# Reordering the start and the pair scalings of a fused retention + Mish MLP kernel on one core

## The chip, the cores and the metric

One NeuronCore of a Trainium2 chip. The metric is the time of one execution on the device in microseconds (us), the median of the fast runs. The mean granted clock of TensorE (1.0 is full speed) is given where it matters. TensorE is called PE, VectorE DVE, ScalarE ACT, GpSimd POOL.

## The reference

```python
# q, k, v: (8, 8, 576, 64) fp32;  moe_w_in (512, 2048), moe_w_out (2048, 512)
scores = (1 / sqrt(64)) * q @ k.transpose(0, 1, 3, 2)
gamma  = 1 - 2.0 ** (-5 - arange(8))                      # one decay per head
rel    = pos[:, None] - pos[None, :]                      # pos = arange(576)
ret    = scores * where(rel >= 0, gamma[:, None, None] ** rel, 0)
x      = (ret @ v) -> (4608, 512)                         # 8 heads x 64 side by side
h      = x @ w_in                                         # "G1"
g      = h * tanh(softplus(h))                            # Mish
out    = g @ w_out                                        # "G2"
```

## The kernel before

The 4608 rows of x are made in 36 chunks of 128, two chunks a pair. For a chunk the kernel scales q and k by powers of the decay (step P, DVE, two TENSOR_TENSORs), transposes them on PE and copies them out of PSUM, the memory that PE writes its results to (T), multiplies q by k and masks (S), multiplies by v and casts into `xT` (O). For the first two pairs k is also turned back on PE into `ks` (`step_n`), and products of k and v are summed up from chunk to chunk (`step_k`) for later O steps. In calls of `first`, q and k stand for scaling, Q and K for the transposes with their copy, V for a cast of v. Four chunks are a tile t: `g1(t, f)` makes one of 16 groups of h and ACT takes Mish of it into `gT`; `g2(t, i)` is a quarter of one chunk's product with w_out. The first four chunks take another way (`first`), with the rows of four tokens on one partition, because it lets the loads start earlier. Chunks 0 to 15 are transposed on PE; the later ones by DMA, and nothing of that part changes. The attention steps stand between the G1 and G2 groups by hand: the program order on each engine is the order of the calls. PSUM has two `sc` buffers of 4 KB, one `st`, two `hp` of 2 KB (all of G1, some of G2) and one `ops` of 2 KB.

```python
def turn_first(n, i):                       # transposes of q (i=0) or k (i=1) of chunk n
    ...
    if n < NCH - 1:
        tp = ps_h.tile([P, 4, P], BF16, name="hp")
    else:                                   # chunk 3: q and k are two parts of one sc tile
        if "tp" not in r:
            r["tp"] = ps_sc.tile([P, 4, NP, P], BF16, name="sc")
        tp = r["tp"][:, 2 * i]
    ... 4 transposes ...
    nc.scalar.copy(r["qk"][:, i, u]..., tp...)

def step_t(n):                              # transposes of chunk n: 4 of q, 4 of k, one tile
    ...
    tp = ps_sc.tile([P, 4, NP, P], BF16, name="sc")[:, 0:2]
    for i in range(2):
        ... nc.tensor.transpose(tp[:, i, p, :], flat[:, ts(p, P)], ident)
    nc.scalar.copy(r["qk"][:, :, u], tp)

def g2(t, i):                               # hp or ops takes the result; DVE copies it to res
    s, part = divmod(i, 4)
    ...
        if t == nT - 1 and s % 2 == 0 or (t, s) in ((0, 1), (0, 3), (1, 1)):
            outs[t] = ps_h.tile([P, d_model], F32, name="hp")
        else:
            outs[t] = ps_o.tile([P, d_model], F32, name="ops")
    ...
    if part == 3:
        store(t, s, ops, nc.vector.tensor_copy)

def visit(m, w):                            # pair m (4 to 7) spread over 8 groups, w = 0 to 7
    n = 2 * m
    if w == 0:
        step_p(m)
        if 2 * m + 2 < NPE: load(m + 4)
    elif w == 2: ...; one(n, "T")
    elif w == 3: one(n + 1, "T")
    elif w == 5: one(n, "S"); one(n + 1, "S")
    elif w == 7: step_k(m); one(n, "O"); one(n + 1, "O")

for i in range(nF):                         # visits 4, 5, 6, 7 and what they stand between
    if i >= 8: visit(4, i % 8)
    g2(0, i)
for i in range(8):
    visit(5, i); g2(1, i)
for i in range(nF):
    visit(6 + i // 8, i % 8)
    ...
    g1(2, i)
    if i % 2: g2(1, 8 + i // 2)
```

## Time and profile before

| | before |
|---|---|
| time, median of 3 runs | 320.43 us (319.65 to 320.83) |
| span of the profiled execution | 318.9 us |
| mean granted clock of PE | 1.0 |
| PE busy | 303.3 us |
| PE not busy | 15.6 us, some 6.5 of it before 10 us and after the last matmul |

PE is the engine to watch. A line of a timeline gives start, duration, engine, line of the program, operation, output and inputs, shapes, the number of instructions drawn together, and in brackets how long the engine stood idle before it and what released it. Because the ends of matmuls are modelled, a loss is counted here as in the prediction: the step from one start to the next, less the same step where nothing waits (0.86 us for four 128x512 matmuls, 0.89 for sixteen 128x128, 0.44 for a chunk's eight transposes). The chain that ended last reads in before:

```profile
PE 78%; DMA 9%; DVE 4%; issue 3%; SPq 2%; POOL 2%; ACT 1%; POOLq 0%; DVEq 0%
```

(SPq is SyncE's queue, POOLq and DVEq those of POOL and DVE; "issue" is time in which nothing was waited for that the profile shows.) These shares count the whole length of each step of the chain, and not the time that PE waited: PE itself waited 0.77 us for w_in, at 22.93. The waits of PE for loads, copies and scalings are what the change goes after.

### The profile page before, as it was taken

How to read it: one execution, taken by the hardware profiler on the slowest of the kernel's cores; microseconds unless marked ns; L12 is line 12 of the kernel's file. 1: busy time of each engine (PE TensorE's matmuls, PEld its weight loads, DVE VectorE, ACT ScalarE, POOL GpSimd, SP SyncE). 2: the span in 40 equal slices, each digit the busy share in tenths (PEclk: the TensorE clock that was granted, in tenths of full speed). 3: DMA queues.
4: the chain of work that ended last, by engine and by line, in shares of the span. 5: the costliest groups of instructions: out<-in, count | busy, mean ns of one | idle time of the engine just before them, and what ended most of it. 6: DMA issues, size and time to landing. Idle time of an engine off the chain costs nothing.

```text
span 318.9 us, 6061 instructions
## 1 busy us (share of the span) xinstructions
PE 303.3 (95%) x2607; PEld 159.1 (50%) x2644; DVE 132.9 (42%) x177; ACT 129.3 (41%) x214; POOL 78.5 (25%) x101
## 2 busy tenths in 40 slices
PE   6779899989999999999999999999999999999995
PEld 2346488745555555444545454445454544444444
DVE  6641554047558475444454535353626232001111
ACT  5656666412464542343434343424242432333200
POOL 6676762532440311313121222240000000000000
PEclk9999999999999999999999999999999999999999
DMA  6999999999998594959594959495040400000032
GB/s 169 261 186 219 198 209 221 202 230 194 247 178 104 110 188 101 168 130 177 121 184 114 182 116 194 106 172 127 33 101 33 101 33 35 33 33 35 33 81 84
DMA packets 71946, 43.38 MB, mean 136 GB/s; under 512 B 55664, under 2 KB 63088, under 8 KB 71920
## 3 DMA queue, kind: packets, MB, share of 16 engines
q0 software_dynamic: 43424, 26.22, 55.7%
q1 hardware_dynamic: 28352, 16.65, 20.3%
q8 instruction: 20, 0.33, 0.4%
q10 hardware_dynamic: 144, 0.13, 0.1%
q14 instruction: 6, 0.05, 0.0%
HBM read 36.70 MB, written 9.44 MB: 145 GB/s over the span
## 4 chain that ended last, share of the span: by engine, by line
PE 78%; DMA 9%; DVE 4%; issue 3%; SPq 2%; POOL 2%; ACT 1%; POOLq 0%; DVEq 0%
PE hp L381 31%; PE ops L419 30%; DMA v<-in_v_dram 5%; PE hp L419 3%; PE sc L317 3%; DVE qks L280 3%; DMA w_in_t<-in_moe_w_in_dram 3%; PE hp L404 2%; SPq L137 2%; PE sc L366 2%; PE sc L359 2%; DMA kraw<-in_k_dram 2%; PE st L338 2%; PE sc L296 1%; PE hp L431 1%
## 5 line engine op out<-in xcount | busy, mean ns | idle before, releaser
L383 ACT ACTIVATE gT<-hp 128x512 bf16<-128x512 f32 x122 | 72.9, 598 | 126.1 <-PE hp L381 105.9
L381 PE MATMUL hp<-xT,w_in_t 128*128 128x512 bf16 x460 | 121.2, 380 | 1.1 <-ACT gT L406 0.2
L419 PE MATMUL ops<-w_out_t,gT 128*128 128x512 bf16 x475 | 121.3, 379 | 0.7
L419 PEld LDWEIGHTS <-gT 128*128 128x128 bf16 x560 | 54.2, 98 | 64.7 <-issue 0.8
L439 DVE COPY res<-ops 128x512 f32<-128x512 f32 x30 | 20.8, 692 | 129.7 <-PE ops L419 129.7
L381 PEld LDWEIGHTS <-w_in_t 128*128 128x128 bf16 x488 | 45.2, 98 | 52.3 <-issue 0.6
L320 DVE TENSOR_TENSOR sm<-sc,mask 128x1024 bf16<-128x1024 f32 x36 | 42.6, 1217 | 23.7 <-PE sc L317 23.7
L564 POOL COPY seen<-qkT 1x1 bf16<-1x1 bf16 x10 | 1.8, 177 | 127.0 <-DMA qkT<-qks 127.0
L342 ACT ACTIVATE ssb<-st,diag 128x512 bf16<-128x512 f32 x32 | 20.2, 684 | 15.5 <-PE st L338 15.5
L107 POOL DMA_DIRECT2D qraw<-in_q_dram x16 | 17.2, 1076 | 24.3 <-DVE qks L280 20.3
L370 DVE CAST xT<-sc 128x512 bf16<-128x512 f32 x32 | 20.8, 685 | 5.4 <-PE sc L366 4.5
L280 DVE TENSOR_TENSOR qks<-kraw,gk 128x1024 bf16<-128x1024 f32 (+1 forms) x18 | 19.8, 1098 | 0.0
L280 DVE TENSOR_TENSOR qks<-qraw,gq 128x1024 bf16<-128x1024 f32 (+1 forms) x18 | 19.7, 1096 | 0.0
L107 POOL DMA_DIRECT2D kraw<-in_k_dram x16 | 17.2, 1076 | 6.1 <-DVE sm L320 3.7
L419 PE MATMUL hp<-w_out_t,gT 128*128 128x512 bf16 x77 | 18.3, 379 | 0.4 <-issue 0.3
L107 POOL DMA_DIRECT2D v<-in_v_dram x16 | 17.3, 1086 | 4.2 <-DMA kraw<-in_k_dram 2.5
L297 ACT COPY qkT<-sc 128x1024 bf16<-128x1024 bf16 x12 | 12.2, 1013 | 14.1 <-PE sc L296 13.9
L404 PE MATMUL hp<-xT,w_in_t 128*128 128x128 bf16 x280 | 17.2, 219 | 0.0
L404 PEld LDWEIGHTS <-w_in_t 128*128 128x128 bf16 x280 | 15.8, 98 | 0.7 <-issue 0.2
L366 PE MATMUL sc<-sm,v 128*64 128x128 bf16 x288 | 13.8, 220 | 0.4 <-DVE sm L320 0.4
L406 ACT ACTIVATE gT<-hp 128x512 bf16<-128x512 f32 (+1 forms) x18 | 10.4, 586 | 6.5 <-PE hp L404 6.2
L317 PEld LDWEIGHTS <-qkT 64*128 64x128 bf16 x288 | 8.1, 94 | 9.8 <-issue 5.9
(72 smaller groups left out, 157.1 us busy)
## 6 DMA issues: line engine op xcount, KB each, us to landing
out_dram<-res SPq DMA_DIRECT2D x31, 256.0 KB, 3.4
qraw<-in_q_dram POOLq DMA_DIRECT2D x12, 512.0 KB, 6.2
kraw<-in_k_dram POOLq DMA_DIRECT2D x12, 512.0 KB, 7.5
v<-in_v_dram POOLq DMA_DIRECT2D x12, 256.0 KB, 8.0
qraw<-in_q_dram POOLq DMA_DIRECT2D x8, 256.0 KB, 9.7
kraw<-in_k_dram POOLq DMA_DIRECT2D x8, 256.0 KB, 9.5
w_out_t<-in_moe_w_out_dram POOLq DMA_DIRECT2D x4, 512.0 KB, 11.6
qraw<-in_q_dram SPq DMA_DIRECT2D x8, 128.0 KB, 4.1
```

Of the source, the lines that this page charges most:

```text
L107: nc.gpsimd.dma_start(out=r[x][ds(off, ni)].rearrange("p u h d -> p (u h) d"), in_=src[ds(b, 2), :, ds(i0, ni), :].rearrange("b h p d -> p ...
L280: nc.vector.tensor_tensor(r["qks"][:, i, u], r["qk"[i]][:, u], g, op=OP.mult)
L317: nc.tensor.matmul(sc[:, e, p, :], lhsT=qk[r, 1, u, p, :], rhs=qk[r, 0, u, p, :], start=True, stop=True)
L320: nc.vector.tensor_tensor(sm.rearrange("p e n i -> p (e n) i"), sc.rearrange("p e n i -> p (e n) i"), (mask if len(chunks[n]) == 1 else ma ...
L342: nc.scalar.activation(ssb[:, :, :, e, :], st, AX.Copy, scale=diag[:, e:e + 1])
L366: nc.tensor.matmul(ot[ds(64 * e, 64), p, :], lhsT=vs[:, u, 2 * p + e, :], rhs=sm[:, e, p, :], start=(start and p == 0), stop=True, skip_gr ...
L370: (nc.scalar.copy if t == 0 else nc.vector.tensor_copy)(xts[t][:, :, ts(s, P)], ot)
L381: nc.tensor.matmul(hp, lhsT=w_in_t[:, c, ts(f, P)], rhs=xts[t][:, c, :], start=(c == 0), stop=(c == KC - 1))
L383: nc.scalar.activation(gts[t][:, f, :], hp, AX.Mish)
L404: nc.tensor.matmul(hp[:, j, :], lhsT=w_in_t[:, c, ts(f + j, P)], rhs=xts[t][:, c, ts(s, P)], start=(c == 0), stop=(c == KC - 1))
L419: nc.tensor.matmul(ops, lhsT=gts[t][:, f, ts(s, P)], rhs=w_out_t[:, f, :], start=(f == 0), stop=(f == nF - 1))
L439: copy(ot, ops)
```

## The change

Its intent: PE should find its operands ready. Chunk 3's transposes go ahead of the first G1 groups, with Q copied by ACT and K by DVE; chunks 4 to 7 have their copies split over the two engines; a pair's scaling is issued one visit (eight groups) ahead of its transposes; the second quarter of w_in comes in two loads. The diff, cut to its core:

```diff
+        copy = nc.vector.tensor_copy if n == NCH - 1 and i else nc.scalar.copy     # turn_first
-        nc.scalar.copy(r["qk"][:, :, u], tp)                                       # step_t
+        if n < 2 * NCH:
+            nc.scalar.copy(r["qk"][:, 0, u], tp[:, 0])
+            nc.vector.tensor_copy(r["qk"][:, 1, u], tp[:, 1])
+        else:
+            nc.scalar.copy(r["qk"][:, :, u], tp)
...
-    load_w_in(4, 4)
+    load_w_in(4, 2)
+    load_w_in(6, 2)
...
+    first(3, "q")
     first(2, "S")
     first(1, "O")
-    first(3, "q")
-    keep_warm(4)
+    first(3, "V")
+    keep_warm(3)
     first(2, "O")
-    first(3, "k")
-    steps = {0: "Q", 1: "KV", 2: "S", 4: "O"}
-    for f in range(6):
+    first(3, "kQK")
+    for f in range(4):
         g1_some(0, f, NCH - 1)
-        first(3, steps.get(f, ""))
+        first(3, {0: "S", 2: "O"}.get(f, ""))
     g1_chunk(3, 0)
-    g1_chunk(3, 4, 2)
...                                     # steps of pair 2 one or two groups earlier or later
     def visit(m, w):
         if w == 0:
-            step_p(m)
             if 2 * m + 2 < NPE: load(m + 4)
...
             one(n, "O")
             one(n + 1, "O")
+            if 2 * m + 2 < NPE:
+                step_p(m + 1)
...
-        if i >= 8:
+        if i == 6:
+            step_p(4)
+        elif i >= 8:
             visit(4, i % 8)
         g2(0, i)
...
-        if i == 6:
+        if i == 9:
             step_p(8)
-        elif i == 8:
+        elif i == 11:
             cross(8)
```

More of the change, by code (lines that the diff above doesn't have):

```diff
@@ L262, in turn_first @@
             nc.tensor.transpose(tp[:, t, :], lines[:, ts(t, P)], ident)
-        nc.scalar.copy(r["qk"][:, i, u].rearrange("p n (g t) -> p n g t", t=4),
-                       tp.rearrange("p t (g n) -> p n g t", n=NP))
+        copy = nc.vector.tensor_copy if n == NCH - 1 and i else nc.scalar.copy
+        copy(r["qk"][:, i, u].rearrange("p n (g t) -> p n g t", t=4), tp.rearrange("p t (g n) -> p n g t", n=NP))
     def cast_first(n):
@@ L492 @@
     load(5)
+    first(3, "q")
     first(2, "S")
     first(1, "O")
-    first(3, "q")
-    keep_warm(4)
+    first(3, "V")
+    keep_warm(3)
     first(2, "O")
-    first(3, "k")
-    steps = {0: "Q", 1: "KV", 2: "S", 4: "O"}
-    for f in range(6):
+    first(3, "kQK")
+    for f in range(4):
         g1_some(0, f, NCH - 1)
-        first(3, steps.get(f, ""))
+        first(3, {0: "S", 2: "O"}.get(f, ""))
     g1_chunk(3, 0)
-    g1_chunk(3, 4, 2)
-    for i in range(6, nF):
-        if i == 7:
+    for i in range(4, nF):
+        if i == 5:
             step_n(0)
+        elif i == 7:
+            step_k(0)
         elif i == 9:
-            step_k(0)
-        elif i == 10:
             step_n(1)
@@ L519 @@
             one(4, "O")
-            one(5, "T")
         g1(0, i)
@@ L527 @@
                 if fb == 0:
+                    one(n + 1, "T")
+                elif fb == 1:
                     one(n + 1, "S")
@@ L530 @@
                         step_k(n // 2)
-                elif fb == 1 and n < 6:
+                elif fb == 2 and n < 6:
                     one(n + 2, "P")
-                elif fb == 2:
+                elif fb == 3:
                     one(n + 1, "O")
-                elif fb == 3 and n < 6:
-                    one(n + 2, "T")
             g1_chunk(n, 4 * fb)
```

## The prediction

> **What bounds the kernel now.** I first read the page's busy shares, to see which engine fills the span:
>
> ```profile
> PE 303.3 (95%) x2607; PEld 159.1 (50%) x2644; DVE 132.9 (42%) x177; ACT 129.3 (41%) x214; POOL 78.5 (25%) x101
> ```
>
> TensorE is busy 303.3 of 318.9 us and the change takes no real matmul away, so all it can win is PE idle time: at most 15.6 us, of which some 2.9 lie in the first 10 us and 3.6 after the last matmul, both untouched. The ends of matmuls are modelled (a 128x512 one shows 380 ns, yet four take 0.86 us start to start), which hides up to 0.2 us of each gap; so I count losses as the step from one start to the next, less the step of the same group where nothing waits. The waits of the whole run say that PE never waits long in one place, so I read the timeline of PE, then of the engines it waits for, stage by stage.
>
> The start (timeline, all engines):
>
> ```profile
> 16.99 0.41 PE L366 MATMUL sc<-sm,v 128*64 128x128 bf16 x8
> 18.08 0.81 PE L392 MATMUL hp<-xT,w_in_t 128*128 128x384 bf16 x4 [0.67 <-ACT xT L370]
> ...
> 19.31 0.58 ACT L264 COPY qkT<-sc 128x512 bf16<-128x512 bf16 x1
> ...
> 19.94 0.38 PE L262 MATMUL sc<-ident,qks 128*128 128x128 bf16 x4 [0.18 <-ACT qkT L264]
> ...
> 22.93 0.82 PE L392 MATMUL hp<-xT,w_in_t 128*128 128x384 bf16 x4 [0.77 <-DMA w_in_t<-in_moe_w_in_dram]
> ```
>
> From O(2) (the first line) to the first full G1 group at 26.55 PE has about 7.0 us of work (O 0.35, six 384-column groups at 0.65, two sets of transposes at 0.22, S and O of chunk 3 at 0.33, 24 small matmuls at 0.055) and takes 9.56. Note the fourth line: K's transposes write another half of the tile than the one ScalarE is copying, and still start only when that copy ends (19.31 + 0.58 = 19.89).
>
> Chunks 4 to 7 (timeline, PE and ACT):
>
> ```profile
> 44.06 0.61 PE L296 MATMUL sc<-ident,qks 128*128 128x128 bf16 x8
> ...
> 44.51 1.06 PE L404 MATMUL hp<-xT,w_in_t 128*128 128x128 bf16 x16
> 44.76 1.01 ACT L297 COPY qkT<-sc 128x1024 bf16<-128x1024 bf16 x1
> ...
> 45.83 0.40 PE L317 MATMUL sc<-qkT 64*128 64x128 bf16 x8 [0.27 <-ACT qkT L297]
> ```
>
> Sixteen small matmuls need 0.89 (96 take 5.36), so S could start at 45.40 and starts at 45.83: 0.43 lost to a 1.01 us copy, and the same at 40.00 and 51.28.
>
> The visits (timeline of PE, then of DVE):
>
> ```profile
> 68.80 0.40 PE L296 MATMUL sc<-ident,qks 128*128 128x128 bf16 x4 [0.19 <-DVE qks L280]
> 69.94 0.40 PE L296 MATMUL sc<-ident,qks 128*128 128x128 bf16 x4 [0.74 <-DVE qks L280]
> ...
> 81.04 0.40 PE L296 MATMUL sc<-ident,qks 128*128 128x128 bf16 x4 [0.62 <-DVE qks L280]
> ...
> 89.07 1.89 PE L381 MATMUL hp<-xT,w_in_t 128*128 128x512 bf16 x8
> ```
>
> ```profile
> 87.73 1.29 DVE L370 CAST xT<-sc 128x512 bf16<-128x512 f32 x2 [0.53 <-PE sc L366]
> 89.14 0.69 DVE L439 COPY res<-hp 128x512 f32<-128x512 f32 x1
> 89.75 1.22 DVE L280 TENSOR_TENSOR qks<-qraw,gq 128x1024 bf16<-128x1024 f32 x1
> 90.88 1.22 DVE L280 TENSOR_TENSOR qks<-kraw,gk 128x1024 bf16<-128x1024 f32 x1
> ```
>
> Transposes come two G2 groups (1.73 us) after a scaling of 2.36 us. One chunk's transposes should take 0.44; they take 68.44 to 70.17, 80.02 to 81.28, 91.66 to 92.39 and 105.22 to 106.08: lost 1.29, 0.82, 0.29 and 0.42, together 2.8 us. From 120 us on PE has at most 0.16 idle in 20 us and the program is the same.
>
> **What the Trainium skill says.** "PSUM — Partial Sum Buffer", section "PSUM bank collisions raise a hardware error", says that two engines must not access one bank and quadrant at once, reads against reads included. The split copy of the ordinary transposes reads two halves of one 2 KB bank (2 x 512 bf16), so I take its two copies to be ordered one after the other, not side by side. The trace shows no such pair yet; the wait at 19.94, between halves 2 KB apart, shows that the program keeps even those apart. The same page, "Engine vs sequencer instructions", calls the VectorE queue strict FIFO, which agrees with every DVE line above: what is issued first runs first, needed or not. "VectorE: DVE Perf Modes", section "The perf-mode tier table", caps a copy out of PSUM at two elements per cycle, for 16-bit data in unit steps. The trace agrees: 1024 bf16 in 0.69 us (the ks copy), 512 fp32 also in 0.69, 256 fp32 in 0.42. Hence my estimates: 0.42 for a dense half of 512 bf16, 0.69 for chunk 3's K copy, which steps through the tile.
>
> **The change part by part** (times of before; gains count minus)
>
> *Chunk 3 ahead of G1.* q3 and k3 had long landed (14.0 and 14.9), v3 too (about 16), so scaling q3 before S(2) leaves sm(2) at 17.0 and O(2) with it; the dropped warm-up matmul lies in that wait and is worth nothing. Then: Q transposes 17.35; ScalarE copies xT(2) until 18.03, then Q until 18.52; K transposes wait for that, 18.57 to 18.79; VectorE copies K until 19.7. First G1 group 18.79 (0.7 later than now), S(3) 19.7, two groups to 21.35, O(3) 21.43, one group to 22.4, then the 16 small matmuls after xT(3), 22.55 to 23.45, f=4 and 5 by 25.2 (without the ks transposes now placed between them). That stands against 26.55: -1.4. If K's transposes did not wait for Q's copy it would be -2.5.
>
> *w_in's second quarter in two loads.* One load came 14.76 to 22.88, the one before it landed at 18.5, so half should land near 20.7. But f=4 is now asked for at 23.45, after even the undivided load. The wait of 0.77 goes by the reordering, the split adds nothing, and costs POOL one issue of 0.76 us into a queue with 10 us of backlog: 0.
>
> *Pair 2 in G1.* ks(1) is made one group earlier, so chunk 4 is scaled in time: its transposes lost 0.2 (33.09 to 33.75 against 0.44): -0.2. Chunk 5's transposes leave their place before f=15, where they waited 0.38 for the scaling: -0.4.
>
> *Chunks 4 to 7.* The chain between T and S keeps one small G1 in between. Copy now: ScalarE 0.59, then VectorE 0.05 + 0.42, 1.06 against 1.01. S waits some 0.48 instead of 0.43, three times: +0.15. Side by side it would be -1.3.
>
> *Scaling a visit ahead.* Pair 4's scaling moves to i=6 of G2, pair 5's to the end of visit 4, in good time (pair 5's data landed by 62.6): -1.29, -0.8, -0.29, -0.42 = -2.8.
>
> *What that costs.* At the end of visit 5 pair 6's scaling (2 x 1.13 us) now goes to VectorE ahead of the copy of G2's result, which shares its `hp` buffer with the second group of G1(2). Now: copy 89.14 to 89.83, group at 89.07 + 0.86 = 89.93, just in time. Then: xT until 88.94, scaling until 91.2, copy until 91.9, group at 91.93: +2.0. At visit 4 the buffers differ and nothing waits. At visit 6 the result is in `ops`, needed again 1.7 us later: +0.2. The later cross-transposes (i=11) still land some 3 us before their use.
>
> Sum: -1.4 - 0.2 - 0.4 + 0.15 - 2.8 + 2.0 + 0.2 = -2.45 us: 320.4 becomes 318.0.
>
> **The rivals.** (a) *The author's hope*: copies side by side, K's transposes free of Q's copy, no stall. -1.1, -1.45 and -2.2 more: 313.2, faster by 2.2%. For it speaks that each idle gap is real; against it the wait at 19.94 and the order of DVE's queue. (b) *Only the copies run side by side*: 316.5. (c) *Only the stall fails to come*: 316. It would need VectorE to reach that copy 2 us earlier, and its queue has no room. (d) *The loads become the bound.* DMA is saturated until 90 us, and PE would come 2 to 3 us earlier. Against it: chunk 5's k lands at 33.6 and would be asked for at about 35.5, later loads have 3 us and more. If it bound, the start's gain would vanish: 319.5 to 320. (e) *A new VectorE delay in chunks 4 to 7*, where K's copy joins scaling, mask and xT (42% busy): up to 0.5 us each, 319.5.
>
> **Range and chances.** Mechanisms that I am fairly sure of give -2.45. Cases (b) and (c) bound one side, (d) and (e) the other; before's own runs spread 319.65 to 320.83. So 316.0 to 319.6. Faster by 2% needs less than 314.0, nearly all of (a): 6%. Slower than 326.8 needs a stall that repeats in the steady part, which is unchanged: 2%.
>
> **What would show it.** Right: K transposes of chunk 3 start when Q's copy ends; S of chunks 5 to 7 still waits 0.4 to 0.5, now for VectorE; no PE wait on `qks` at the visits; one PE wait of about 2 us on `res` at the second group of G1(2), near 90. Wrong: ScalarE's and VectorE's halves overlapping in time; no wait on `res`; a PE wait on a load of q, k or w_in after 23 us; a gap in the steady part that was not there.

## The result, and the profile after

| | before | after |
|---|---|---|
| time, median of 4 runs | 320.63 us (319.65 to 320.89) | 316.92 us (316.74 to 317.21) |
| span of the profiled execution | 318.9 us | 315.3 us |
| ratio, 95% interval | | 0.9891 (0.9868 to 0.9914) |

A ratio is the mean time of one kernel's fast runs over that of the other's of the same rounds, so not quite the ratio of the medians quoted. The change saves 3.5 to 3.7 us (1.1%): within 2%, inside the predicted range, and 1.1 us better than predicted. The busy shares and the chain that ended last, after:

```profile
PE 304.6 (97%) x2635; PEld 158.8 (50%) x2635; DVE 134.9 (43%) x182; ACT 127.2 (40%) x212; POOL 78.7 (25%) x102
...
PE 89%; DVE 3%; SPq 2%; DMA 2%; ACT 2%; issue 1%; DVEq 0%
```

PE stands idle 10.7 us instead of 15.6 by the first line, but some of that is only in the count: after shows 2635 matmuls and as many weight loads, before 2607 and 2644, so 37 records of matmuls are missing in before's trace. The steps between starts are safer. DMA fell from 9% of the chain to 2%: the chain no longer runs through the loads of w_in and v, and PE's wait for w_in at 22.93 is gone.

The start (timeline of after, all engines):

```profile
16.67 0.41 PE L370 MATMUL sc<-sm,v 128*64 128x128 bf16 x8 [0.22 <-DVE sm L324]
...
17.60 0.59 ACT L265 COPY qkT<-sc 128x512 bf16<-128x512 bf16 x1
...
18.24 0.38 PE L262 MATMUL sc<-ident,qks 128*128 128x128 bf16 x4 [0.83 <-ACT qkT L265]
...
19.48 0.40 PE L321 MATMUL sc<-qkT 64*128 64x128 bf16 x8 [0.20 <-DVE qkT L265]
...
23.23 1.03 PE L385 MATMUL hp<-xT,w_in_t 128*128 128x512 bf16 x4
...
24.54 1.89 PE L385 MATMUL hp<-xT,w_in_t 128*128 128x512 bf16 x8
```

Group f=6 in before (timeline of before, PE):

```profile
26.55 1.02 PE L381 MATMUL hp<-xT,w_in_t 128*128 128x512 bf16 x3 [0.24 <-ACT gT L406]
```

K's transposes (18.24) do start only when the copy of Q ends (17.60 + 0.59), and the first full group, f=4 at 23.23, waits for no load. The line at 24.54 holds two groups, f=5 and f=6, so f=6 starts 0.86 later, at 25.40; less the 0.44 us of `ks` transposes now placed before it that is 8.29 us from O(2) (the first line), against 9.56 before (26.55 less 16.99): -1.27.

Chunks 4 to 7 (timeline of after, all engines; chunk 6 stands for three):

```profile
43.24 1.06 PE L408 MATMUL hp<-xT,w_in_t 128*128 128x128 bf16 x16
...
43.49 0.59 ACT L298 COPY qkT<-sc 128x512 bf16<-128x512 bf16 x1
...
44.11 0.42 DVE L299 COPY qkT<-sc 128x512 bf16<-128x512 bf16 x1 [1.42 <-ACT qkT L298]
...
44.59 0.40 PE L321 MATMUL sc<-qkT 64*128 64x128 bf16 x8 [0.30 <-DVE qkT L299]
```

The two copies come one after the other: DVE was idle for 1.42 us and was released by ACT's copy. S starts 1.35 us after the sixteen matmuls that need 0.89: 0.46 lost, 0.43 before.

The visits (timeline of after, PE):

```profile
66.35 0.61 PE L296 MATMUL sc<-ident,qks 128*128 128x128 bf16 x8
...
76.65 0.62 PE L296 MATMUL sc<-ident,qks 128*128 128x128 bf16 x8
...
84.90 1.02 PE L385 MATMUL hp<-xT,w_in_t 128*128 128x512 bf16 x4
86.61 1.02 PE L385 MATMUL hp<-xT,w_in_t 128*128 128x512 bf16 x4 [0.69 <-ACT gT L387]
...
88.33 0.61 PE L296 MATMUL sc<-ident,qks 128*128 128x128 bf16 x8
...
101.16 1.02 PE L423 MATMUL ops<-w_out_t,gT 128*128 128x512 bf16 x4 [0.25 <-DVE res L443]
```

All transposes of a chunk are now in one line of eight with no wait on `qks`: each set takes 0.44 to 0.46. Two new waits stand at 86.61 and 101.16. The first is where a wait of 2 us for DVE was predicted; it is shorter, and it is for ACT. The lines of DVE and ACT beside it (timeline of after, all engines):

```profile
84.76 1.22 DVE L280 TENSOR_TENSOR qks<-qraw,gq 128x1024 bf16<-128x1024 f32 x1
...
85.89 1.22 DVE L280 TENSOR_TENSOR qks<-kraw,gk 128x1024 bf16<-128x1024 f32 x1
...
85.96 0.60 ACT L387 ACTIVATE gT<-hp 128x512 bf16<-128x512 f32 x1 [1.58 <-PE hp L385]
...
87.03 0.69 DVE L443 COPY res<-hp 128x512 f32<-128x512 f32 x1
```

DVE does scale pair 6 ahead of the result's copy, and that copy ends only at 87.72. But the second G1 group began at 86.61, before it: so it cannot be that copy that it waited for. It starts when Mish of the first group ends (85.96 + 0.60).

| part | before to after, by starts | predicted | measured |
|---|---|---|---|
| O(2) itself starts earlier | 16.99 to 16.67 | - | -0.32 |
| O(2) to f=6, without the ks transposes | 9.56 to 8.29 | -1.4 | -1.27 |
| chunk 4's transposes | 0.66 to 0.44 | -0.2 | -0.22 |
| chunks 4 to 7, up to the first G2 group | | -0.4 + 0.15 | -0.30 |
| transposes of visits 4, 5, 6, 7 | | -2.8 | -1.29, -0.80, -0.28, -0.41 |
| second group of G1(2) | 0.86 to 1.71 | +2.0 | +0.85 |
| G2 group at 101.16 | | +0.2 | +0.41 |
| sum | span 318.9 to 315.3 | -2.45 | -3.63 |

I take the first row for chance: the change makes nothing faster that O(2) waits for, and in the traces of before, after and the kernels below O(2) starts anywhere between 16.4 and 17.1, as the loads land.

### The profile page after: what moved, and what is told of

Its sections match the earlier page's. It is cut to its first block, busy times and chain, and to the rows that moved or that the text cites. A ratio compares the mean times of both kernels' runs of the same rounds, so it can differ in the third digit from the quotient of the medians.

```text
span 315.3 us, 6082 instructions
## 1 busy us (share of the span) xinstructions
PE 304.6 (97%) x2635; PEld 158.8 (50%) x2635; DVE 134.9 (43%) x182; ACT 127.2 (40%) x212; POOL 78.7 (25%) x102
## 4 chain that ended last, share of the span: by engine, by line
PE 89%; DVE 3%; SPq 2%; DMA 2%; ACT 2%; issue 1%; DVEq 0%
PE hp L385 34%; PE ops L423 33%; PE hp L423 6%; PE hp L408 4%; PE sc L321 3%; PE sc L370 2%; PE sc L363 2%; SPq L137 2%; PE st L342 2%; DMA kraw<-in_k_dram 2%; PE sc L296 1%; PE hp L435 1%; DVE sm L324 1%; PE hp L396 1%; ACT qkT L298 0%
## 5 line engine op out<-in xcount | busy, mean ns | idle before, releaser
L385 PE MATMUL hp<-xT,w_in_t 128*128 128x512 bf16 x496 | 126.6, 380 | 0.7 <-ACT gT L387 0.7
L387 ACT ACTIVATE gT<-hp 128x512 bf16<-128x512 f32 x124 | 74.2, 599 | 128.5 <-PE hp L385 128.3
L107 POOL DMA_DIRECT2D kraw<-in_k_dram x16 | 17.1, 1070 | 10.5 <-issue 4.9
L410 ACT ACTIVATE gT<-hp 128x512 bf16<-128x512 f32 x17 | 10.2, 598 | 7.0 <-PE hp L408 6.8
L321 PE MATMUL sc<-qkT 64*128 64x128 bf16 x288 | 11.9, 218 | 1.1 <-DVE qkT L299 0.9
```

What stands on the lines that cost most here:

```text
L107: nc.gpsimd.dma_start(out=r[x][ds(off, ni)].rearrange("p u h d -> p (u h) d"), in_=src[ds(b, 2), :, ds(i0, ni), :].rearrange("b h p d -> p ...
L321: nc.tensor.matmul(sc[:, e, p, :], lhsT=qk[r, 1, u, p, :], rhs=qk[r, 0, u, p, :], start=True, stop=True)
L385: nc.tensor.matmul(hp, lhsT=w_in_t[:, c, ts(f, P)], rhs=xts[t][:, c, :], start=(c == 0), stop=(c == KC - 1))
L387: nc.scalar.activation(gts[t][:, f, :], hp, AX.Mish)
```

## The experiments

Ten kernels ran, all correct. They ran in three sets: two of four kernels, in each of which the kernel before had a median of 320.43 us (11 runs), and a last one of two (experiments 9 and 10) with 320.05 (9 runs). A ratio is to the kernel before of the same set. "After" in a diff is the changed kernel; it did not run again in these sets, so "better than after" compares times of different sets, between which the kernel before itself differs by up to 0.6 us.

### 1. Which buffer the second G1 group waits for

Theory: `hp` is two buffers, but they are not handed out strictly in turn. The addresses in the built program of after (read from the program, not from a trace) show the first and the second G1 group of tile 2 in the same one, and G2's result in the other; in before they alternate. So the second group must wait for Mish of the first, and is spared the copy of G2's result. Then forcing the turn must bring the predicted wait back. The rival: ACT's Mish was late by itself, and the buffer makes no difference.

```diff
 # on after
-    ps_h = ctx.enter_context(tc.tile_pool(name="ps_h", bufs=2, space=PS))
+    # two pools of one buffer each; every hp tile takes the other one
+    hps = [ctx.enter_context(tc.tile_pool(name=f"ps_h{i}", bufs=1, space=PS)) for i in range(2)]
...                                     # a small class hands out the other pool at each call
```

> The changed kernel with the two hp buffers taken strictly in turn. In its trace the second G1 group of the third token block took the buffer of the first and lost 0.85 us (84.90 to 86.61 against 0.86), where I had forecast 2.0 us of waiting for the copy of G2's result. Theory: the 2.0 was right for buffers in turn and failed only because the program picked the other buffer. Then this run shows a PE wait on res of about 2.0 us there, and is 1.1 us slower than the changed kernel: 318.0. Rival: VectorE's queue delays the copy less than I reckoned, and buffers don't matter: within 0.2 us of the changed kernel, 316.9.

Measured: 318.29 us (318.08 to 319.53, 6 runs), ratio 0.994 (0.992 to 0.996). Timeline of this kernel, all engines:

```profile
84.60 1.02 PE L390 MATMUL hp<-xT,w_in_t 128*128 128x512 bf16 x4
...
86.73 0.69 DVE L448 COPY res<-hp 128x512 f32<-128x512 f32 x1
...
87.47 1.49 PE L390 MATMUL hp<-xT,w_in_t 128*128 128x512 bf16 x4 [1.85 <-DVE res L448]
```

The step is 2.87 instead of 0.86: 2.01 us lost, for `res`, where the prediction had 2.0. The theory holds; the rival falls.

The second group also took longer (1.49 instead of 1.02). The table by stretches of the same kernel (columns: stretch, its length, busy time and count of each engine, granted clock, DMA share, GB/s) shows why:

```profile
86.00:87.40 1.40, 0.00 (x0) 0.00 (x0) 1.40 (x2) 0.26 (x1) 1.25 (x2) 1.00 1.07 323
88.40:91.00 2.60, 2.60 (x12) 1.20 (x11) 0.00 (x0) 0.60 (x1) 1.21 (x2) 0.50 1.70 197
91.40:91.60 0.20, 0.20 (x4) 0.08 (x2) 0.00 (x0) 0.09 (x1) 0.00 (x0) 1.00 1.34 276
```

PE was granted half its clock from about 87.9 to 91.3 us. In it two groups of four took 1.28 and 1.71 (0.86 otherwise) and a set of transposes 0.85 (0.44): another 1.7 us. That execution is the slowest of the six (319.53, mean clock 0.993); the others took 318.08 to 318.51, at clocks of 0.995 to 1.0 and the two at 0.995 fastest. They are 1.0 to 1.5 us faster, so this loss seems to belong to the one execution; theirs have no trace that would show it. The forced turn by itself should cost 2.0 less 0.85, 1.15 us; the medians are 1.4 apart.

### 2. Pair 6's scaling back behind the result's copy

If pair 6's scaling is all that delays the group, putting it back must remove the wait and give back visit 6's gain.

```diff
 # on after, in visit
+            if m == 6: step_p(m)                      # w == 0, as in before
-            if 2 * m + 2 < NPE:                       # w == 7
+            if 2 * m + 2 < NPE and m != 5:
                 step_p(m + 1)
```

> The changed kernel with only pair 6's scaling back behind the copy of G2's result (as before the change). Theory: the 0.85 us at the second G1 group goes, and the 0.28 us that the transposes of chunk 12 lost comes back: 0.6 us faster than the changed kernel, 316.3. Rival: the 0.85 us comes from elsewhere (ScalarE's queue): no faster, and 0.3 slower for the transposes, 317.2.

Measured: 316.71 us (316.32 to 316.83, 5 runs), ratio 0.9883 (0.9864 to 0.9901). Timeline, PE:

```profile
85.25 1.89 PE L385 MATMUL hp<-xT,w_in_t 128*128 128x512 bf16 x8
...
87.83 0.89 PE L296 MATMUL sc<-ident,qks 128*128 128x128 bf16 x8
88.56 0.81 PE L385 MATMUL hp<-xT,w_in_t 128*128 128x512 bf16 x3
```

Eight matmuls in one line: the wait is gone, and the transposes take 0.73 again, 0.29 lost. By the trace that is 0.56 us better than after; the times show 0.2, between the two expectations, and the ranges of the runs overlap (after: 316.74 to 317.21). O(2) started 0.35 later in this trace than in after's, and three of its five runs had a clock of 0.994 to 0.998. The mechanism is shown; the size is not settled by this run.

### 3. The scalings of pairs 6 and 7 in a gap of DVE

A place that should pay for neither: right after the second chunk's transposes of the visit before.

```diff
 # on after, in visit
         elif w == 3:
             one(n + 1, "T")
+            if m in (5, 6):
+                step_p(m + 1)
...                                                     # w == 7
-            if 2 * m + 2 < NPE:
-                step_p(m + 1)
+            if m == 4:
+                step_p(5)
```

> The changed kernel with the scalings of pairs 6 and 7 issued in the middle of the visit ahead (after its second transposes), where VectorE stood idle 2.1 and 5.5 us, instead of at its end. Theory: both stalls of the result's copy go (0.85 at the second G1 group of block 3, 0.41 at G2 near 101 us), and the transposes still do not wait: 1.2 us faster than the changed kernel, 315.7. Rival: the scaling now delays masks, xT or another result copy, and PE pays there: 316.5 to 317.5.

Measured: 315.8 us (315.44 to 315.84, 4 runs), ratio 0.9853 (0.9829 to 0.9878): 1.1 better than after. Timeline, all engines:

```profile
84.89 1.89 PE L385 MATMUL hp<-xT,w_in_t 128*128 128x512 bf16 x8
...
84.96 0.69 DVE L443 COPY res<-hp 128x512 f32<-128x512 f32 x1
```

The result's copy now ends at 85.65, before the second group needs a buffer; there is no wait there, none at the G2 group of visit 6, and the transposes at 87.48 take 0.45. Against after that returns the 0.85 and the 0.41, 1.26 us, of which the times show 1.1.

### 4. One copy by ScalarE instead of two halves

```diff
 # on after, in step_t
-        if n < 2 * NCH:
-            nc.scalar.copy(r["qk"][:, 0, u], tp[:, 0])
-            nc.vector.tensor_copy(r["qk"][:, 1, u], tp[:, 1])
-        else:
-            nc.scalar.copy(r["qk"][:, :, u], tp)
+        nc.scalar.copy(r["qk"][:, :, u], tp)
```

> The changed kernel with the split copy undone: ScalarE alone copies Q and K of chunks 4 to 7 in one 1.01 us instruction. Theory: the two halves run one after the other (ScalarE 0.59, then VectorE 0.42), so S waits 0.43 instead of 0.46 in chunks 5 to 7: same time, 316.8 within 0.2. Rival: the split copy pays: S waits longer by 0.3 to 0.5 in each of three chunks, 317.9 to 318.4.

Measured: 317.14 us (316.76 to 317.21, 5 runs), ratio 0.9896 (0.9878 to 0.9915), not to be told from after's 316.92. S waits 0.25 to 0.27 us, on ACT, where in after it waits 0.28 to 0.30, on DVE. The split as written is worth nothing either way.

### 5. One load of w_in's second quarter

```diff
 # on after
-    load_w_in(4, 2)
-    load_w_in(6, 2)
+    load_w_in(4, 4)
```

> The changed kernel with w_in's second quarter again in one load. Theory: f=4 is asked for at 23.2 us, just after the undivided load lands (22.6 to 22.9), so nothing changes: 316.9 within 0.2, no PE wait on w_in above 0.1. Rival: the split is what took the 0.77 us wait away: PE waits 0.4 to 0.8 on w_in at f=4 and the time is 317.3 to 317.7.

Measured: 317.1 us (316.54 to 317.68, 4 runs), ratio 0.989 (0.9873 to 0.9908): the same as after. Group f=4 starts at 23.45 and waits for no load, so the splitting is worth nothing once chunk 3 goes first.

### 6. The visits' part alone, on before

```diff
 # on before: only the hunks in visit and in the three loops around it
```

> The kernel before with only the scalings of the visits moved ahead (and the crossing moved from i=8 to 11). Theory: 1.29 + 0.80 + 0.28 + 0.41 gained at the transposes of chunks 8, 10, 12, 14, 0.85 and 0.41 lost at the copies of the results: 1.5 us faster than before, 319.1. Rival: the parts depend on each other (the visits gain only because the start came earlier): under 0.7 us.

Measured: 318.82 us (318.41 to 319.4, 6 runs), ratio 0.9946 (0.9932 to 0.996): -1.6. By steps it should be -2.78 + 0.85 + 0.41 = -1.52. Here too the second group waits for Mish of the first (0.75 us idle, released by ACT).

### 7. The start alone, on before

```diff
 # on before: chunk 3 ahead of G1, K's copy on DVE, w_in's second quarter in two loads
```

> The kernel before with only the start changed: chunk 3's scaling, transposes and two-engine copy ahead of G1, four narrow groups instead of six, w_in's quarter in two loads. Theory: K's transposes wait for Q's copy, and the start wins 1.3 to 1.5 us, which the rest keeps: 319.1. Rival: loads bind further on and take it back: 320 or more, with PE waits on loads after 25 us.

Measured: 319.05 us (318.78 to 319.22, 5 runs), ratio 0.995 (0.9937 to 0.9964): -1.4, as predicted for this part. With experiment 6 that makes -3.0 of the -3.5; the other 0.5 fits that of chunks 4 to 7 in the table (-0.22 and -0.30), a part that did not run alone.

### 8. K's transposes of chunks 4 to 7 in a PSUM tile of their own

If the two copies follow each other because both read one tile, two tiles let them overlap. The `ops` buffer is free at that time.

```diff
 # on after, in step_t
+        tk = ps_o.tile([P, NP, P], BF16, name="ops") if n < 2 * NCH else None
-                nc.tensor.transpose(tp[:, i, p, :], flat[:, ts(p, P)], ident)
+                nc.tensor.transpose(tk[:, p, :] if i and n < 2 * NCH else tp[:, i, p, :], ...)
-            nc.vector.tensor_copy(r["qk"][:, 1, u], tp[:, 1])
+            nc.vector.tensor_copy(r["qk"][:, 1, u], tk)
```

> The changed kernel with K's transposes of chunks 4 to 7 in a PSUM tile of their own (the ops bank, idle in that stage), nothing else. Theory: the copies of Q and K went one after the other only because both read one tile; apart they overlap, and S of chunks 5, 6 and 7 waits under 0.1 instead of 0.46: 1.2 us faster than the changed kernel, 315.7. Rival: ScalarE and VectorE hinder each other, or S waits for the Mish of the small group ahead of it: under 0.4 us faster.

Measured: 316.03 us (315.74 to 316.26, 4 runs), ratio 0.9857 (0.9839 to 0.9876): 0.9 better than after. Timeline, all engines:

```profile
42.77 1.06 PE L409 MATMUL hp<-xT,w_in_t 128*128 128x128 bf16 x16
42.97 0.42 DVE L300 COPY qkT<-ops 128x512 bf16<-128x512 bf16 x1 [0.75 <-PE ops L297]
43.02 0.58 ACT L299 COPY qkT<-sc 128x512 bf16<-128x512 bf16 x1
...
43.76 0.40 PE L322 MATMUL sc<-qkT 64*128 64x128 bf16 x8
```

The copies overlap, S waits for neither, and the step is 0.99: 0.1 lost instead of 0.46, three times over. Both copies still write the same `qkT` tile, so it is the PSUM source that ordered them in after. A further kernel, with the halves in two banks of one tile, was built and not run: its program still has the wait between the two copies. The trace of after shows the same for a copy and transposes: chunk 3's halves lie 2 KB apart, so in two banks, and K's transposes still waited 0.83 us for Q's copy (18.24). So the program keeps apart what touches one tile, whatever the bank. Whether the chip would bear two such reads of one bank was not tried.

### 9. The same for chunk 3

```diff
 # on after, in turn_first, chunk 3
-            if "tp" not in r:
-                r["tp"] = ps_sc.tile([P, 4, NP, P], BF16, name="sc")
-            tp = r["tp"][:, 2 * i]
+            tp = ps_o.tile(... name="ops") if i else ps_sc.tile(... name="sc")[:, 0]
```

> The changed kernel with K's transposes of chunk 3 in a PSUM tile of their own. Theory: in the changed kernel they wait 0.83 us for ScalarE's copy of Q, because both lie in one tile; apart they follow Q's at once, the first G1 group starts some 0.7 us earlier and S needs no wait: 1.0 us faster than the changed kernel, 315.9. Rival: PE then reaches w_in's next part before it has landed, and the gain goes into a wait on a load: under 0.3 us.

Measured: 316.38 us (315.85 to 316.46, 4 runs), ratio 0.9879 (0.9861 to 0.9897): 0.5 better than after by the times, which alone do not show a gain: the kernel before was 0.4 to 0.6 us faster in this set too, and the interval of the ratio overlaps that of after (0.9868 to 0.9914). The trace shows it. Timeline, PE:

```profile
17.08 0.41 PE L371 MATMUL sc<-sm,v 128*64 128x128 bf16 x8 [0.22 <-DVE sm L325]
...
17.68 0.40 PE L263 MATMUL ops<-ident,qks 128*128 128x128 bf16 x4
...
22.65 1.03 PE L386 MATMUL hp<-xT,w_in_t 128*128 128x512 bf16 x3
```

K's transposes (17.68) start without a wait, ahead of ScalarE's copy of Q (18.01 in the timeline of ACT), and from O(2) to f=4 it takes 5.57 us, 6.56 in after: 1.0 saved inside this stretch, as expected. But O(2) itself came 0.41 later than in after's trace, which is most of the missing half. That it is chance fits the spread of O(2) over the traces; it was not shown by itself.

### 10. The three improvements together

After with the edits of experiments 3, 8 and 9.

> The changed kernel with all three: K apart in chunk 3, K apart in chunks 4 to 7, scalings of pairs 6 and 7 in the middle of the visit ahead. Theory: the gains add, 1.0 + 1.2 + 1.2: 313.5, 2.2% faster than the kernel before. Rival: earlier PE runs into loads of q and k at chunk 5 (landed at 33.6 in the kernel before, asked for near 34): 314.5 or more, with a VectorE wait on a load there.

Measured: 313.92 us (313.53 to 313.98, 5 runs), ratio 0.9805 (0.9789 to 0.9822) to before's 320.05: 6.1 us less, and 3.0 less than after by the times, 2.8 by the ratios. Whether that is 2% stays unclear, as the interval spans 0.98. The sum of the parts would be -3.5 -1.1 -0.9 and between -0.5 and -1.0. No load became the bound: the first G2 group, at 55.41, is 4.4 us earlier than in before (0.6 of it because O(2) was). This is the best version, and better than both kernels.

## Why the prediction was right, and where it was not

- **Start, -1.4.** Right: -1.27 in the trace, -1.4 alone on the chip (experiment 7). Its reason, that K's transposes wait for Q's copy, is seen at 18.24, and the 1.1 it said that this costs measured 1.0 by the trace of experiment 9. Its estimates of the copies on DVE, 0.42 for K's half of chunks 4 to 7 and 0.69 for chunk 3, were both measured (44.11 and 18.73). One sum was wrong: the work named between O(2) and f=6 adds up to 6.7 us, and not to "about 7.0"; the -1.4 does not rest on it.
- **w_in in two loads, 0.** Right (experiment 5): the reordering removed the wait for the load, not the splitting.
- **Pair 2, -0.2, and chunk 5's transposes, -0.4, with +0.15 for the copies.** Right: -0.22 and -0.30. The copies came one after the other; the loss of 0.46 a chunk was put at 0.48. Experiment 4 finds no gain in the split.
- **Scaling a visit ahead, -2.8.** Right: -2.78.
- **The wait for G2's result, +2.0.** Wrong in size and in what was waited for, and this is where the 1.1 us between 318.0 and 316.9 come from: 1.15 less than predicted. That the number shows it so neatly is luck, for the other differences (+0.13 at the start, +0.21 at visit 6, -0.32 of O(2) and smaller ones) cancel. The step that failed: "the copy of G2's result, which shares its `hp` buffer with the second group of G1(2)". DVE's queue ran as written there. But in the program of after the two G1 groups had one buffer and the result the other, so the group lost 0.85 us, waiting for Mish. One of the prediction's own signs of being wrong, no wait on `res` there, came true. I had read the alternation in before and taken it as given for after. With strict turns 2.01 us are lost (experiment 1). Rival (c) in the prediction named a time of 316 without this wait, but for another reason: it asked for an earlier DVE, and DVE was not earlier.
- **Visit 6, +0.2.** Predicted too small by half: 0.41, and here the wait was on `res` as it said (101.16).
- **The rivals.** (a) and (b) needed copies side by side, and the change as written did not bring them; (d) did not happen, not even with 6 us less (experiment 10); (e) is not seen, S losing 0.46 instead of 0.43.

The author's hope of 313.2 in rival (a) was a fair reading of what lay there: three small edits, each of which takes away one cause of waiting that the prediction named, reach 313.9.

## What to carry to other kernels

When work is moved ahead on an in-order engine, look at what then stands behind it: the place after another step in the gap of the same engine cost nothing, the place ahead of a copy that frees PSUM cost 1.1 us. Splitting a copy over two engines pays only if the halves lie in tiles that the program does not order (0.9 us here, against nothing). And before a wait on a buffer is predicted, read from the built program which buffer each tile was given; a schedule that is moved can get other ones.

## What the Trainium skill lacked or had wrong

- "TensorE: Matmul & The Clock Gate", Part 1, lets the clock fall to half after at least one idle window of about 3.4 us, and its closing table advises against idle gaps over some 3 us. In experiment 1 PE had stood still for 1.85 us by the profile and was at work again from 87.47, when the granted clock fell to 0.50, at about 87.9 us. In the trace of experiment 7 it fell at about 7.5 us, after idle times of 0.42 and 1.36 us with four transposes between. Both times half the clock lasted 3.4 us, which agrees with the page's window. So here the clock fell after shorter gaps than these two passages name, in some executions and not in others; why is not shown. The page's section "A second HAM failure mode: psum-queue depth-cycling" does tell of frequent short idle times between groups of matmuls; what it lacks is how short, and a case like experiment 1, where one gap of 1.85 us came before a loss of 1.7 us.
- "PSUM — Partial Sum Buffer", "PSUM bank collisions raise a hardware error", gives the bank and quadrant as what must be kept apart. It lacks that the waits in a program can be coarser: here they keep whole tiles apart, two banks or one. Transposes into one bank of a tile waited 0.83 us for a copy out of its other bank (18.24 in after), and not at all with a tile of their own (17.68 in experiment 9). The two copies of chunks 4 to 7 do not tell tile from bank: out of halves of one tile, which lie in one bank, they took 1.04 us from the first start to the last end (43.49 to 44.53), and 0.63 out of two tiles in two banks (42.97 to 43.60).
- No page of those drawn on has that a pool of two buffers need not hand them out in turn. Here it cost 0.85 us where strict turns would have cost 2.0.
